# Linear attention and SwiGLU block: q kept transposed, z by one-column matmuls, the reciprocal denominators broadcast through DRAM

## The chip, the cores and the metric

The kernel runs on one core of a Trainium2 chip. The metric is the device time in microseconds (us) of one execution; smaller is better. Inside a core, TensorE (PE) multiplies matrices into PSUM, VectorE (DVE), ScalarE (ACT) and GpSimd (POOL) do the elementwise work, and the queue of SyncE (SP) issues the DMAs. Each engine takes its instructions in program order and waits on semaphores for the others.

## The reference

S = 2048 tokens, D = 1024, 32 heads of 32, F = 3584; all tensors are bfloat16.

```python
mod = (silu(c) @ w_mod).reshape(1, 6, 1, -1)      # sa, ca, ga, sb, cb, gb
h = layernorm(x) * (1 + ca) + sa
q, k, v = split(h @ wqkv)                          # 32 heads of 32
phi = lambda t: where(t > 0, t + 1, exp(t)) + 1e-06
pq, pk = phi(q), phi(k)
kv  = einsum('bhsd,bhse->bhde', pk, v)
z   = einsum('bhsd->bhd', pk)                      # sum of pk over the tokens
num = einsum('bhqd,bhde->bhqe', pq, kv)
den = einsum('bhqd,bhd->bhq', pq, z) + 1e-06
x = x + ga * ((num / den) @ wo)
h = layernorm(x) * (1 + cb) + sb
x = x + gb * ((silu(h @ w_gate) * (h @ w_up)) @ w_down)
```

## The kernel before

Tokens come in 16 tiles of 128 (`NST`) and four chunks of 512 (`NCH`); D comes in eight tiles of 128 (`NDT`, `NHG`; one `hg` holds four heads). The order of the work is written out by hand: calls append instructions to each engine's list, dependences are found from the addresses, and each engine runs its list in order. All instructions are recorded by one helper, so every row of the profile has line L178 and has to be told apart by its tiles.

**Chunk 0** computes q in eight groups (`q_phase_chunk0`, line 623), then k in eight. Each group is eight matmuls into one PSUM bank and then `phi_evac` (line 556): ACT writes exp (`E1`, tile e) and relu (`RL`, tile rl), DVE takes min and adds (two instructions). Between the k groups of chunk 0 PE transposes chunk 1's normalised rows (`th_round`, line 459), four rounds with two ACT evacuations each.

**Chunks 1 to 3** (`chunk`, line 681) run 16 groups each. A table `side` hangs further work behind each group: the LayerNorm statistics, `ln1_rstd` and `ln1_xn` of a coming chunk (DVE, POOL), its DMA transposes into `HT` (`th_dma`, line 469), its modulation on ACT (`th_mod`, line 474, tile ht), and one-column matmuls of w_mod (`mod_col_mm`, line 594) whose result `mod_col_fin` spreads (`MODREP`) and `mod_bcast` (line 612) multiplies out to all partitions. `zacc` (line 585) adds each k tile to `PKSUM` in fp32 on DVE; after chunk 3 `PKSUM` is split into `ZHI` and `ZLO`, and four matmuls with a matrix of ones give `ZB`, z on all partitions.

**The G stage** (lines 816 to 849) computes G = xn^T · pk in 16 groups of 16 matmuls over four PSUM banks (`g_group`, 2 to 5), each evacuated by `g_evac` (ACT scales z into `GTMP`, DVE adds). Beside it the denominators of 16 token tiles are made, one per group: `den_prod` multiplies q by `ZB` on POOL, `den_scale` on DVE sums 32 columns each, adds 1e-6, takes the reciprocal, multiplies q by it, and has a DMA transpose q into `PQT`. `fold_ga` (DVE) multiplies `WO` by ga. `kvt_mm` makes v^T·k per head from G (PE, masked by DVE into `KVT`), `m_mm` multiplies it with `WO` into `MW`; both come in two halves, the second behind the last G group.

**The wo stage** (`wo_part`, `wo_res`, lines 804 to 902) multiplies `PQT` with `MW` for 16 token tiles and adds x, which is loaded again behind the G stage (`xr` DMAs, since `XRES` held the normalised rows). **The SwiGLU stage** follows.

Of the kernel before, what the change touches and what calls it, by code (L numbers as in the profile page):

```python
# [264 lines left out]
def bass_adaLN_cond__linear_attn_block__swiglu_ffn__prompt_kernel(  # L265
# [22 lines left out]
    with ExitStack() as es:  # L288
# [15 lines left out]
        PQ = T("pq", 32 * KB, [128, NST, D], BF16)  # L304
        WMSC = T("wmsc", 32 * KB, [128, NDT, 2048], BF16)
        AT = T("at", 32 * KB, [128, NFT, 512], BF16)
# [20 lines left out]
        DEN = T("den", SM + 2304, [128, 2, 32], FP32)  # L327
        RECIP = T("recip", SM + 2560, [128, 2, 32], FP32)
# [5 lines left out]
        PQT = T("pqt", 72 * KB, [128, NHG, S], BF16)  # L334
# [10 lines left out]
        PKSUM = T("pksum", 192 * KB, [128, D], FP32)  # L345
        ZHI = T("zhi", 184 * KB, [128, D], BF16)
        ZLO = T("zlo", 186 * KB, [128, D], BF16)
        GTMP = T("gtmp", 184 * KB, [128, 2, 512], FP32)
        KVT = T("kvt", 188 * KB, [128, NHG, 128], BF16)
        ZB = T("zb", 196 * KB, [128, D], FP32)  # L350
        PROD = [T("prod0", 192 * KB, [128, D], FP32), T("prod1", 200 * KB, [128, D], FP32)]
        WD_A = T("wd_a", 72 * KB, [128, 16, D], BF16)
# [14 lines left out]
        PS = nc.alloc_psum_tensor("ps", [128, 8, 512], FP32)  # L367
        PSB = PS.bitcast(BF16)

# [39 lines left out]
        for h in range(4):  # L409
            P.dve("memset", ap=MASK[32 * h:32 * h + 32, 32 * h:32 * h + 32], constant=1.0)  # L410

# [3 lines left out]

        def xnat(st):
            return XRES[:, st, :]
# [51 lines left out]
        def th_dma(ch):  # L469
            buf = ch % 2  # L470
            for j in range(4):
                xbar(HT[:, buf, :, j * 128:(j + 1) * 128], XRES[:, 4 * ch + j, :])
# [92 lines left out]
        def q_part(g, bank, dts):  # L565
            h, j = g // 4, g % 4
            for dt in dts:
                P.pe("matmul", out=PS[:, bank, :], lhsT=HT[:, 0, dt, j * 128:(j + 1) * 128],
                     rhs=WQK[:, dt, h * 512:(h + 1) * 512], start=(dt == 0), stop=(dt == NDT - 1))
# [4 lines left out]
        def qk_group(ch, j, isk, h):  # L574
            st = 4 * ch + j
            buf = ch % 2
            bank = QK_BANKS[qk_ctr[0] % 5]
            qk_ctr[0] += 1
            lo = isk * D + h * 512
# [3 lines left out]
            phi_evac(bank, PKH[h][:, st, :] if isk else PQ[:, st, h * 512:(h + 1) * 512])  # L583

        def zacc(st, h):
            dst = PKSUM[:, h * 512:(h + 1) * 512]
            if st == 0:
                P.dve("tensor_copy", out=dst, in_=PKH[h][:, st, :])
            else:
                P.dve("tensor_tensor", out=dst, in0=dst, in1=PKH[h][:, st, :], op=ALU.add)  # L590
# [3 lines left out]
        def mod_col_mm(piece, kt):  # L594
            c0 = 8 * piece
            for m in range(NDT):
                P.pe("matmul", out=PS[:, 6, c0 + m:c0 + m + 1], lhsT=STG[:, kt, m * 128:(m + 1) * 128],
                     rhs=SILUC[:, kt:kt + 1], start=mcol_first[0], stop=(kt == NDT - 1), skip_group_check=True)
                mcol_first[0] = False
# [23 lines left out]
        def q_phase_chunk0(side):  # L623
# [18 lines left out]
            for g in range(7):  # L642
                q_part(g, 1 + g, hi)
                phi_evac(1 + g, PQ[:, g % 4, (g // 4) * 512:(g // 4 + 1) * 512])
                for f in side.get(g, []):
                    f()
            q_part(7, 1, lo + hi)
            phi_evac(1, PQ[:, 3, 512:1024])
# [14 lines left out]
        for jj in range(4):  # L663
            add(kside, jj // 2, lambda jj=jj: ln1_xn(4 + jj))
        for r in range(4):
            add(kside, 3 + r, lambda r=r: th_round(1, r, 7 if r % 2 == 0 else 6, "act"))
        q_phase_chunk0(qside)
        gi = 0
        for h in range(2):
            for j in range(4):  # L670
                qk_group(0, j, 1, h)
# [3 lines left out]
            for j in range(4):  # L675
                add(kside, 100 + h, lambda j=j, h=h: zacc(j, h))
        for h in range(2):
            for f in kside[100 + h]:
                f()

        def chunk(ch, side):
            gi = 0
            for j in range(4):
                st = 4 * ch + j
                for (isk, h) in [(0, 0), (1, 0), (0, 1), (1, 1)]:
                    qk_group(ch, j, isk, h)
                    for f in side.get(gi, []):
                        f()
                    if isk:
                        zacc(st, h)  # L690
                    gi += 1
# [20 lines left out]
        for i, f in enumerate(ops):  # L712
            add(s1, 8 + (i * 2) // 3, f)
# [4 lines left out]
        add(s2, 0, lambda: ln1_rstd(3))  # L718
        for jj in range(4):
            add(s2, 1 + jj // 2, lambda jj=jj: ln1_xn(12 + jj))  # L720
        add(s2, 2, lambda: th_dma(3))
        for dt in range(NDT):
            add(s2, 8 + dt, lambda dt=dt: th_mod(3, dt))
        piece_mm(s2, 1, 0)
        add(s2, 7, lambda: mod_col_fin(1, 3, False, False))
        add(s2, 7, lambda: stg_load(2))
        piece_mm(s3, 2, 0)
        add(s3, 7, lambda: mod_col_fin(2, 2, True, False))
        add(s3, 7, lambda: stg_load(3))
# [29 lines left out]
        def den_prod(st):  # L759
            P.pool("tensor_tensor", out=PROD[st % 2][:], in0=PQ[:, st, :], in1=ZB[:], op=ALU.mult)  # L760

        def den_scale(st):
            i = st % 2
            P.dve("tensor_reduce", out=DEN[:, i, :], in_=PROD[i][:].rearrange("p (h e) -> p h e", e=32),
                  axis=mybir.AxisListType.X, op=ALU.add)
            P.dve("tensor_scalar", out=DEN[:, i, :], in0=DEN[:, i, :], scalar1=1e-6, scalar2=None, op0=ALU.add)
            P.dve("reciprocal", out=RECIP[:, i, :], in_=DEN[:, i, :])
            P.dve("tensor_tensor", out=PQ[:, st, :].rearrange("p (h e) -> p h e", e=32),
                  in0=PQ[:, st, :].rearrange("p (h e) -> p h e", e=32),
                  in1=RECIP[:, i, :].unsqueeze(2).to_broadcast([128, 32, 32]), op=ALU.mult)  # L770
            xbar(PQT[:, :, st * 128:(st + 1) * 128], PQ[:, st, :])

# [42 lines left out]

        g_group(0)
        for h in range(2):
# [171 lines left out]
```

## Time and profile before

| | |
|---|---|
| three runs | 895.74 us median (895.6 to 896.42) |
| the profiled execution, own time | 895.89 us |
| its span, first to last instruction | 894.1 us |
| mean granted TensorE clock | 0.977 |
| SwiGLU stage | from 311.2 us to the end |

The trace is of one execution. Its view by windows gives the busy time of each engine in a stretch, its timeline each instruction's start and length with the idle time before it and what ended that, its groups the mean length of one instruction of a kind, and its DMA list the time from issue to landing. "Granted clock" is the share of the full TensorE clock that the chip allowed.

### The profile page before, as it was taken

To read this page: it belongs to the slowest core of one execution; us is meant where nothing else is said; L and a number is where in the kernel's file an instruction comes from. 1 tells how busy PE (TensorE), PEld (TensorE's weight loads), DVE (VectorE), ACT (ScalarE), POOL (GpSimd) and SP (SyncE) were. 2 spreads that over 40 slices of the span, in tenths; PEclk is the share of its full clock that TensorE was granted. 3 is DMA by queue.
4 is the path that set the end of the run, shared out by engine and by line. 5 is a ranking of instruction groups with operands and counts; after the bars stand their busy time and mean duration, and the time that the engine had idled before them with its cause. 6 is when DMAs were issued, how large, how long until landed. Compare 5 with 4: busy or idle time off the path is not lost.

```text
span 894.1 us, 10474 instructions
## 1 busy us (share of the span) xinstructions
PE 843.3 (94%) x4289; PEld 391.3 (44%) x4289; DVE 329.5 (37%) x638; ACT 220.2 (25%) x375; POOL 69.2 (8%) x66
## 2 busy tenths in 40 slices
PE   4897899966779999999999999999999999999998
PEld 3453345433334444444444444444444444444444
DVE  4658655699975422121112121112212111212111
ACT  4664685311123321111111111111111111111101
POOL 1000000333300300002000000200000200000000
PEclk9988999997979999999999999999999999999999
DMA  9924432312255779655025556204555602554000
GB/s 302 376 76 100 84 101 95 107 36 57 42 138 154 196 239 306 187 142 152 22 61 141 156 164 158 64 18 134 154 142 145 150 24 59 143 162 119 1 24 24
DMA packets 185233, 110.80 MB, mean 124 GB/s; under 512 B 44896, under 2 KB 170848, under 8 KB 185184
## 3 DMA queue, kind: packets, MB, share of 16 engines
q1 hardware_dynamic: 185184, 110.12, 44.0%
q8 instruction: 34, 0.56, 0.3%
q14 instruction: 15, 0.12, 0.0%
HBM read 95.42 MB, written 4.19 MB: 111 GB/s over the span
## 4 chain that ended last, share of the span: by engine, by line
PE 80%; DVE 9%; issue 5%; ACT 4%; DMA 1%; SPq 0%; POOL 0%; DVEq 0%; ACTq 0%
PE ps L178 80%; DVE den L178 2%; ACT e_89 L178 1%; ACT ht L178 1%; ACT rl L178 1%; DMA wmsc<-in_w_mod_dram 1%; DVE g L178 1%; DVE stats L178 1%; DVE pksum L178 1%; DVE recip L178 1%; DVE wo L178 1%; DVE pq L178 1%; DVE xres L178 1%; DVE mw L178 0%; DVE e_89 L178 0%
## 5 line engine op out<-in xcount | busy, mean ns | idle before, releaser
L178 DVE TENSOR_TENSOR at<-sg,ps 128x512 bf16<-128x512 bf16 x112 | 77.0, 687 | 300.0 <-PE ps L178 298.3
L178 ACT ACTIVATE sg<-ps 128x512 bf16<-128x512 f32 x112 | 66.9, 597 | 310.5 <-PE ps L178 310.5
L178 PE MATMUL ps<-wqk,ht 128*128 128x512 bf16 x512 | 124.4, 395 | 3.3 <-ACT ht L178 3.3
L178 PE MATMUL ps<-wd_a,at 128*128 128x512 bf16 (+2 forms) x528 | 115.9, 373 | 0.0
L178 PE MATMUL ps<-wd_b,at 128*128 128x512 bf16 (+2 forms) x396 | 88.3, 373 | 0.0
L178 PEld LDWEIGHTS ps<-wd_a,at 128*128 128x128 bf16 x528 | 51.1, 98 | 59.8
L178 PEld LDWEIGHTS ps<-wqk,ht 128*128 128x128 bf16 x512 | 49.2, 101 | 61.9 <-issue 8.4
L178 DVE TENSOR_TENSOR ut<-att,gb_b 128x512 bf16<-128x512 bf16 (+1 forms) x32 | 14.5, 454 | 164.8 <-ACT att L178 164.8
L178 ACT ACTIVATE att<-ps 128x512 bf16<-128x512 f32 (+1 forms) x32 | 19.0, 594 | 179.7 <-PE ps L178 179.7
L178 PE MATMUL ps<-mw,pqt 128*128 128x512 bf16 x256 | 57.0, 383 | 1.0 <-DVE xres L178 1.0
L178 PEld LDWEIGHTS ps<-wd_b,at 128*128 128x128 bf16 x396 | 38.3, 98 | 44.7
L178 POOL TENSOR_SCALAR h2t<-h2t,modcol 128x512 bf16<-128x512 bf16 x32 | 25.0, 797 | 394.6 <-DMA h2t<-xn_110 394.6
L178 PE MATMUL ps<-h2t,gug_102 128*128 128x512 bf16 x224 | 52.9, 379 | 0.0
L178 PE MATMUL ps<-h2t,guu_106 128*128 128x512 bf16 x224 | 52.9, 379 | 0.0
L178 PE MATMUL ps<-h2t,gug_103 128*128 128x512 bf16 x224 | 52.9, 379 | 0.0
L178 PE MATMUL ps<-h2t,guu_108 128*128 128x512 bf16 x224 | 52.9, 379 | 0.0
L178 PE MATMUL ps<-h2t,gug_105 128*128 128x512 bf16 x224 | 52.9, 379 | 0.0
L178 PE MATMUL ps<-h2t,guu_109 128*128 128x512 bf16 x224 | 52.9, 379 | 0.0
L178 PE MATMUL ps<-h2t,guu_107 128*128 128x512 bf16 x224 | 52.9, 379 | 0.0
L178 PE MATMUL ps<-h2t,gug_104 128*128 128x512 bf16 x224 | 52.9, 379 | 0.0
L178 ACT ACTIVATE e_89<-ps 128x512 bf16<-128x512 f32 x64 | 38.6, 603 | 40.5 <-PE ps L178 30.9
L178 DVE TENSOR_TENSOR pq<-pq,recip 128x1024 bf16<-128x1024 bf16 x16 | 40.6, 2536 | 0.6
(104 smaller groups left out, 716.3 us busy)
## 6 DMA issues: line engine op xcount, KB each, us to landing
stg<-in_w_mod_dram SPq DMA_DIRECT2D x4, 2048.0 KB, 8.0
gug_102<-in_B_w_gate_dram SPq DMA_DIRECT2D x14, 512.0 KB, 3.9
guu_106<-in_B_w_up_dram SPq DMA_DIRECT2D x14, 512.0 KB, 5.1
gug_103<-in_B_w_gate_dram SPq DMA_DIRECT2D x14, 512.0 KB, 4.0
guu_107<-in_B_w_up_dram SPq DMA_DIRECT2D x14, 512.0 KB, 5.2
gug_104<-in_B_w_gate_dram SPq DMA_DIRECT2D x14, 512.0 KB, 3.9
guu_108<-in_B_w_up_dram SPq DMA_DIRECT2D x14, 512.0 KB, 5.2
gug_105<-in_B_w_gate_dram SPq DMA_DIRECT2D x14, 512.0 KB, 3.9
```

The source lines that it names most:

```text
L178: return getattr(e, method)(**kw)
```

## The change

Five parts belong together. `PQT` becomes the place where q is computed: in `q_group` the weight `WQK` is the stationary operand and `HT` the moving one, so q comes out transposed, and `phi_evac` writes it there; `PQ` and 16 DMA transposes go. z becomes 128 one-column matmuls (`z_mm`, `PKH` against a column of ones, into PSUM bank 6), in place of `zacc`; `z_bcast` spreads it to all partitions. `den` computes all denominators with 32 matmuls of 32 output rows each (`ZSEL` picks the four heads of a group), one add, one reciprocal and one cast on DVE, writes 32x2048 reciprocals to a DRAM scratch (four DMAs), waits for them on SP, and reads them back spread over the partitions into `RB` (four DMAs of 1 MB in SBUF). `scale_pq` multiplies `PQT` by `RB` in eight DVE instructions. The chunks do their eight k groups first and then the eight q groups, and the LayerNorm work, transposes and modulation get other places in the side tables. `AT` and `WD_A` change places in SBUF with it.

```diff
-        def th_dma(ch):
...
+        def th_dma(st):
+            buf, j = (st // 4) % 2, st % 4
+            xbar(HT[:, buf, :, j * 128:(j + 1) * 128], XRES[:, st, :])
...
+        def q_group(ch, nt):
+            buf, bank = ch % 2, next_bank()
+            for dt in range(NDT):
+                P.pe("matmul", out=PS[:, bank, :], lhsT=WQK[:, dt, nt * 128:(nt + 1) * 128],
+                     rhs=HT[:, buf, dt, :], start=(dt == 0), stop=(dt == NDT - 1))
+            phi_evac(bank, PQT[:, nt, ch * 512:(ch + 1) * 512])
...
-        def zacc(st, h):
...
+        def z_mm(st):
+            for hg in range(NHG):
+                P.pe("matmul", out=PS[:, 6, 32 + hg:33 + hg], lhsT=PKH[hg // 4][:, st, (hg % 4) * 128:(hg % 4 + 1) * 128],
+                     rhs=ONES[:, 0:1], start=mcol_first[0], stop=(st == NST - 1), skip_group_check=True)
                 mcol_first[0] = False
...
-            add(kside, jj // 2, lambda jj=jj: ln1_xn(4 + jj))
+            add(kside, 1 + jj // 2, lambda jj=jj: ln1_xn(4 + jj))
         for r in range(4):
-            add(kside, 3 + r, lambda r=r: th_round(1, r, 7 if r % 2 == 0 else 6, "act"))
+            add(kside, 4 + r, lambda r=r: th_round(1, r, 7 if r % 2 == 0 else 6, "act"))
...
         def chunk(ch, side):
-            gi = 0
-            for j in range(4):
-                st = 4 * ch + j
-                for (isk, h) in [(0, 0), (1, 0), (0, 1), (1, 1)]:
-                    qk_group(ch, j, isk, h)
...
-                    if isk:
-                        zacc(st, h)
-                    gi += 1
+            for gi in range(16):
+                if gi < 8:
+                    k_group(ch, gi // 2, gi % 2)
+                else:
+                    q_group(ch, gi - 8)
+                for f in side.get(gi, []):
+                    f()
...
+        for j in range(4):
+            add(s1, 1 + j, lambda j=j: z_mm(j))
+            for ch, s_ in ((1, s1), (2, s2), (3, s3)):
+                add(s_, 4 + 2 * j, lambda st=4 * ch + j: z_mm(st))
...
-            add(s1, i // 2, f)
-        add(s1, 6, lambda: ln1_rstd(2))
+            add(s1, (i * 5) // 12, f)
+        add(s1, 4, lambda: ln1_rstd(2))
         for jj in range(4):
             add(s1, 6 + jj // 2, lambda jj=jj: ln1_xn(8 + jj))
-        add(s1, 7, lambda: th_dma(2))
-        for dt in range(NDT):
-            add(s1, 12 + dt // 2, lambda dt=dt: th_mod(2, dt))
+            add(s1, 6 + jj // 2, lambda jj=jj: th_dma(8 + jj))
+        for i, dt in zip([10, 11, 11, 12, 12, 13, 13, 14], range(NDT)):
+            add(s1, i, lambda dt=dt: th_mod(2, dt))
...
-        add(s1, 7, lambda: mod_col_fin(0, None, False, True))
-        add(s1, 7, lambda: stg_load(1))
-        add(s1, 9, lambda: mod_bcast(GA_B))
...
+        add(s1, 8, lambda: mod_col_fin(0, None, False, True))
+        add(s1, 8, lambda: stg_load(1))
+        add(s1, 13, lambda: mod_bcast(GA_B))
...
-            add(s2, 8 + dt, lambda dt=dt: th_mod(3, dt))
+            add(s2, 7 + dt, lambda dt=dt: th_mod(3, dt))
...
-            add(s3, 12 + kt // 2, lambda kt=kt: mod_col_mm(3, kt))
-        add(s3, 15, lambda: mod_col_fin(3, None, False, True))
+            add(s3, 14 + kt // 4, lambda kt=kt: mod_col_mm(3, kt))
...
-        P.dve("tensor_copy", out=ZHI[:], in_=PKSUM[:])
-        P.dve("tensor_tensor", out=ZLO[:], in0=PKSUM[:], in1=ZHI[:], op=ALU.subtract)
+        P.dve("tensor_copy", out=ZCOL[:], in_=PS[:, 6, 32:40])
+        P.dve("tensor_copy", out=ZHL[:, 0, :], in_=ZCOL[:])
+        P.dve("tensor_tensor", out=ZHL[:, 1, :], in0=ZCOL[:], in1=ZHL[:, 0, :], op=ALU.subtract)
...
+        for i in range(2):
+            P.dve("tensor_copy", out=ZREP[:, i, :, :], in_=ZHL[:, i, :].unsqueeze(2).to_broadcast([128, NHG, 128]))
+        mod_col_fin(3, None, False, True)
...
+        def z_bcast():
+            for h in range(2):
+                for hl in range(4):
+                    for i in range(2):
+                        P.pe("matmul", out=PS[:, h, hl * 128:(hl + 1) * 128], lhsT=ZREP[:, i, 4 * h + hl, :],
+                             rhs=IDENT[:], start=(hl == 0 and i == 0), stop=(i == 1), skip_group_check=True)
+                P.act("activation", out=ZB[:, h * 512:(h + 1) * 512], in_=PS[:, h, :], func=ACT.Copy)
+
+        def den():
+            for hg in range(NHG):
+                for ch in range(NCH):
+                    P.pe("matmul", out=PS[32 * ch:32 * ch + 32, 7, :], lhsT=ZSEL[:, hg * 32:hg * 32 + 32],
+                         rhs=PQT[:, hg, ch * 512:(ch + 1) * 512], start=(hg == 0), stop=(hg == NHG - 1),
+                         skip_group_check=True)
+            P.dve("tensor_scalar", out=DEN[:], in0=PS[:, 7, :], scalar1=1e-6, scalar2=None, op0=ALU.add)
+            P.dve("reciprocal", out=RCP[:], in_=DEN[:])
+            P.dve("tensor_copy", out=RCB[:], in_=RCP[:])
+            wr = [P.dma("rdr%d" % ch, RDR[:, ch * 512:(ch + 1) * 512], RCB[32 * ch:32 * ch + 32, :])
+                  for ch in range(NCH)]
+            P.wait_for("sp", wr)
+            for hh in range(4):
+                src = RDR.rearrange("(g x) s -> x g s", x=4)[hh].unsqueeze(0).to_broadcast([32, NHG, S])
+                P.dma("rb%d" % hh, RB[32 * hh:32 * hh + 32, :, :], src)
+
+        def scale_pq(hg):
+            P.dve("tensor_tensor", out=PQT[:, hg, :], in0=PQT[:, hg, :], in1=RB[:, hg, :], op=ALU.mult)
...
+        z_bcast()
         g_group(0)
...
         g_evac(0)
-        mod_bcast(GB_B)
-        den_prod(0)
+        den()
         for g in range(1, 16):
             g_group(g)
             g_evac(g)
-            if g < 15:
-                den_prod(g)
-            den_scale(g - 1)
...
+            if g == 2:
+                mod_bcast(GB_B)
+            if 3 <= g <= 6:
+                fold_ga(2 * g - 6)
+                fold_ga(2 * g - 5)
+            if g == 9:
                 kvt_mm(0)
...
+            if 11 <= g <= 14:
+                m_mm(g - 11, [0, 1, 7])
+            if 8 <= g <= 15:
+                scale_pq(g - 8)
```

On PE, at the k groups of chunk 0, before (`ident,xres` are the transposes of chunk 1's rows; eight rows `wqk,ht` are one group, the first row of 80 ends with four k groups):

```order
L178 MATMUL ps<-wqk,ht 128x512 x80
L178 MATMUL ps<-ident,xres 128x128 x8
L178 MATMUL ps<-wqk,ht 128x512 x8
L178 MATMUL ps<-ident,xres 128x128 x8
L178 MATMUL ps<-wqk,ht 128x512 x8
L178 MATMUL ps<-ident,xres 128x128 x8
L178 MATMUL ps<-wqk,ht 128x512 x8
L178 MATMUL ps<-ident,xres 128x128 x8
L178 MATMUL ps<-wqk,ht 128x512 x16
L178 MATMUL ps<-siluc,stg 128x1 x8
```

and now (`ht,wqk` is a q group):

```order
L178 MATMUL ps<-ht,wqk 128x512 x48
L178 MATMUL ps<-wqk,ht 128x512 x40
L178 MATMUL ps<-ident,xres 128x128 x8
L178 MATMUL ps<-wqk,ht 128x512 x8
L178 MATMUL ps<-ident,xres 128x128 x8
L178 MATMUL ps<-wqk,ht 128x512 x8
L178 MATMUL ps<-ident,xres 128x128 x8
L178 MATMUL ps<-wqk,ht 128x512 x8
L178 MATMUL ps<-ident,xres 128x128 x8
L178 MATMUL ps<-wqk,ht 128x512 x8
```

Five k groups stand ahead of the first round instead of four, and none stands behind the last round: the row that follows it is chunk 1's first group, which reads what that round transposed.

On PE, from the end of chunk 3 into the G stage, before (`siluc,stg` are one-column matmuls of w_mod, `pk,xres` G groups):

```order
L178 MATMUL ps<-siluc,stg 128x1 x16
L178 MATMUL ps<-pk_84,xres 128x512 x16
L178 MATMUL ps<-zhi,ones 128x512
L178 MATMUL ps<-zlo,ones 128x512
L178 MATMUL ps<-zhi,ones 128x512
L178 MATMUL ps<-zlo,ones 128x512
L178 MATMUL ps<-ident,modrep 128x128 x8
L178 MATMUL ps<-pk_84,xres 128x512 x112
L178 MATMUL ps<-pk_85,xres 128x512 x16
L178 MATMUL ps<-g,wv 128x128 x32
```

and now (`ident,zrep` is `z_bcast`, `pqt,zsel` is `den`):

```order
L178 MATMUL ps<-siluc,stg 128x1 x32
L178 MATMUL ps<-ident,zrep 128x128 x16
L178 MATMUL ps<-pk_85,xres 128x512 x16
L178 MATMUL ps<-pqt,zsel 32x512 x32
L178 MATMUL ps<-pk_85,xres 128x512 x32
L178 MATMUL ps<-ident,modrep 128x128 x8
L178 MATMUL ps<-pk_85,xres 128x512 x80
L178 MATMUL ps<-pk_86,xres 128x512 x32
L178 MATMUL ps<-g,wv 128x128 x32
```

The spreading of z moved from behind the first G group to ahead of it, the 32 denominator matmuls are new, and the first `g,wv` (kvt_mm) stands behind ten G groups instead of nine.

On DVE, in the G stage, before (the work of one of the early groups; the later ones lack the two `wo` rows):

```order
L178 SCALAR_TENSOR_TENSOR g<-ps,modcol,gtmp 128x512
L178 TENSOR_REDUCE den<-prod_99 128x32
L178 TENSOR_SCALAR den<-den 128x32
L178 RECIPROCAL recip<-den 128x32
L178 TENSOR_TENSOR pq<-pq,recip 128x1024
L178 TENSOR_TENSOR wo<-wo,ga_b 128x1024 x2
```

and now, from the evacuations of groups 7 and 8 on (counted from 0):

```order
L178 SCALAR_TENSOR_TENSOR g<-ps,modcol,gtmp 128x512 x2
L178 TENSOR_TENSOR pqt<-pqt,rb 128x2048
L178 SCALAR_TENSOR_TENSOR g<-ps,modcol,gtmp 128x512
L178 TENSOR_TENSOR kvt<-ps,mask 128x512
L178 TENSOR_TENSOR pqt<-pqt,rb 128x2048
L178 SCALAR_TENSOR_TENSOR g<-ps,modcol,gtmp 128x512
```

Four denominator instructions per group are gone; one multiplication of 2048 columns stands behind each of the last eight evacuations, and the first of them stands ahead of the mask of kvt.

More of the change, by code (lines that the diff above doesn't have):

```diff
@@ L641, in q_phase_chunk0 @@
             q_part(6, 7, lo)
[L642 to L645, printed above, removed]
+            for nt in range(7):
+                q_part(nt, 1 + nt, hi)
+                phi_evac(1 + nt, PQT[:, nt, 0:512])
+                for f in side.get(nt, []):
                     f()
             q_part(7, 1, lo + hi)
-            phi_evac(1, PQ[:, 3, 512:1024])
+            phi_evac(1, PQT[:, 7, 0:512])
             for f in side.get(7, []):
@@ L814, in wo_res @@
                   op1=ALU.add, accum_out=SUMXH[:, st, nh:nh + 1])
+        z_bcast()
         g_group(0)
-        for h in range(2):
-            for (zt, s0, s1_) in [(ZHI, True, False), (ZLO, False, True)]:
-                P.pe("matmul", out=PS[:, h, :], lhsT=ONES[:], rhs=zt[:, h * 512:(h + 1) * 512], start=s0, stop=s1_)
-            P.act("activation", out=ZB[:, h * 512:(h + 1) * 512], in_=PS[:, h, :], func=ACT.Copy)
         g_evac(0)
-        mod_bcast(GB_B)
-        den_prod(0)
+        den()
         for g in range(1, 16):
```

108 lines of the change are left out of this document (41 added, 67 removed).

## The prediction

> **What bounds the kernel now.** I read the page's engine line first, then the windows cut at the stages, then PE's waits.
>
> ```profile
> PE 843.3 (94%) x4289; PEld 391.3 (44%) x4289; DVE 329.5 (37%) x638; ACT 220.2 (25%) x375; POOL 69.2 (8%) x66
> core 0: us, PE busy (x) PEld busy (x) DVE busy (x) ACT busy (x) POOL busy (x), PEclk, DMA share, GB/s
> 58.41:98.70 40.29, 32.72 (x201) 15.18 (x200) 33.74 (x80) 23.71 (x42) 1.01 (x1) 0.92 0.34 79
> 193.30:208.50 15.20, 3.61 (x33) 3.10 (x32) 14.89 (x18) 2.17 (x3) 5.67 (x3) 0.65 0.27 52
> 311.17:894.10 582.93, 580.39 (x2717) 264.54 (x2715) 113.98 (x197) 88.29 (x147) 20.02 (x25) 1.00 0.43 119
> PE ps L178 <- DVE g L178: 20.6, 5, 4.9
> PE ps L178 <- DVE modrep L178: 5.0, 1, 5.0
> PE ps L178 <- ACT ht L178: 3.3, 6, 1.3
> ```
>
> PE at 94% is an average that hides two places. From 311 us to the end PE has almost no gap, and the change adds nothing there: those 583 us stay. From 193 to 208 us, in the G stage, DVE is busy for 14.9 of 15.2 us and PE for 3.6; PE waits 20.6 us in all for DVE's evacuations of G. In chunk 1 (58 to 99 us) DVE is busy for 33.7 of 40.3 us, and PE waits 5.0 us for `MODREP`.
>
> ```profile
> 175.72 0.74 DVE L178 SCALAR_TENSOR_TENSOR g<-ps,modcol,gtmp 128x512 bf16<-128x512 f32 x1
> 176.38 1.20 DVE L178 TENSOR_REDUCE den<-prod_99 128x32 f32<-128x1024 f32 x1
> 178.23 2.73 DVE L178 TENSOR_TENSOR pq<-pq,recip 128x1024 bf16<-128x1024 bf16 x1
> 182.08 0.74 DVE L178 SCALAR_TENSOR_TENSOR g<-ps,modcol,gtmp 128x512 bf16<-128x512 f32 x1
> 165.70 24.34 PE L178 MATMUL ps<-pk_84,xres 128*128 128x512 bf16 x112
> 189.87 3.62 PE L178 MATMUL ps<-pk_85,xres 128*128 128x512 bf16 x16
> ```
>
> From one evacuation to the next DVE takes 6.36 us. PE takes (189.87 - 165.70) / 112 = 0.216 us per matmul, 3.45 per group. PE runs ahead through its four banks until `kvt_mm` wants the last evacuations; then it stands.
>
> **G stage -17.5, tail -13.2.**
>
> ```profile
> 54.51 0.61 PE L178 MATMUL ps<-ident,xres 128*128 128x128 bf16 x8
> 54.95 3.62 PE L178 MATMUL ps<-wqk,ht 128*128 128x512 bf16 x16
> 238.56 1.89 PE L178 MATMUL ps<-mw,pqt 128*128 128x512 bf16 x8
> 311.17 1.89 PE L178 MATMUL ps<-h2t,gug_102 128*128 128x512 bf16 x8
> ```
>
> Behind 165.70 stand 240 G matmuls (51.8 us), 32 of `kvt_mm` at (54.95 - 54.51) / 8 = 0.055 (1.8) and eight of `m_mm` (1.7): 55.3 us of work in the 72.9 up to 238.56, so 17.5 lost, to waits and to the lowered clock that they bring (0.65 above). From 238.56 to 311.17, 72.6 us, stand 256 wo matmuls, 32 and eight: 58.8. I leave 0.6 for bank and mask waits between the last `m_mm`; 13.2 go.
>
> They go only if DVE keeps up and `RB` is there in time.
>
> ```profile
> L178 DVE TENSOR_TENSOR wo<-wo,ga_b 128x1024 bf16<-128x1024 bf16 x8 | 5.1, 679 | 0.0
> L178 DVE RECIPROCAL recip<-den 128x32 f32<-128x32 f32 x16 | 5.6, 353 | 0.6
> L178 DVE TENSOR_SCALAR den<-den 128x32 f32<-128x32 f32 x16 | 2.9, 182 | 0.6
> L178 DVE CAST mw<-ps 128x512 bf16<-128x512 f32 x8 | 5.5, 685 | 2.7 <-PE ps L178 2.6
> stg<-in_w_mod_dram SPq DMA_DIRECT2D x4, 2048.0 KB, 8.0
> out_dram<-xres SPq DMA_DIRECT2D x31, 128.0 KB, 1.7
> 254.29 2.00 SPq L178 DMA_DIRECT2D xres<-in_A_x_dram  x4
> ```
>
> DVE, groups 8 to 15: evacuation 0.74, `scale_pq` of 2048 columns at 2 x 0.68 = 1.4 (same form as the `wo` row; at most 2 x 2.73, the `pq` row, which ran beside POOL's products, and these are gone), a cast 0.69: 2.8 of 3.45. Groups 3 to 6: 0.74 + two `fold_ga`, 2.1. So DVE has room; at 2.7 per `scale_pq` the four groups with a cast would cost 0.7 each, 2.7 in all.
>
> `RB`: the reciprocal of 512 columns is 0.69 + 512 x (353 - 182) / 32 ns = 3.4 us (between 0.69 and 16 x 0.353 = 5.6). Add before it 0.7 and cast behind it 0.4 make 4.5. Four write issues at 0.5 and a landing of 1.7 (SP stands in its wait; behind it are only the `RB` loads and the x loads, which wait for the last G group anyway) make 3.7. The loads write 4.2 MB: at 2 MB in 8.0 us, 16.0. Together 24.2 us behind `den`. `scale_pq(0)` comes up after groups 1 to 8, the GB broadcast and one evacuation, 28.8 behind `den`; and PE feels a late one only at `m_mm(0)`, whose mask stands behind it on DVE, 9.4 us later. Hidden, with 14 us to spare; the loads may take 29 us.
>
> **The denominators: +6.9.** No row has a 32-row matmul. Matmul time in the rows follows the moving columns (0.216 for 512, 0.055 for 128), so 32 of 512 columns cost 6.9; if the four of one set, which write different quarters of a bank, ran side by side, 8 x 0.216 = 1.7. I take the upper end, the row's own pace; both ends stay in the range.
> The Trainium skill, "TensorE: Matmul & The Clock Gate", Part 3 on packing small matmuls, states that matmuls with 32 output rows in different column groups run at the same time, three of them 2.38 times as fast. No run here shows it yet; an estimate from that page is 6.9 / 2.38 = 2.9.
>
> **z: +3.2, and the wait for it +2.1 and +1.7.**
>
> ```profile
> 60.33 0.34 PE L178 MATMUL ps<-siluc,stg 128*128 128x1 bf16 x8
> 60.54 1.89 PE L178 MATMUL ps<-wqk,ht 128*128 128x512 bf16 x8
> 159.17 0.60 ACT L178 ACTIVATE e_89<-ps 128x512 bf16<-128x512 f32 x1 [1.04 <-PE ps L178]
> 160.63 0.16 DVE L178 CAST modtmp<-ps 128x8 bf16<-128x8 f32 x1
> 160.82 0.69 DVE L178 COPY modrep<-modtmp 128x1024 bf16<-128x1024 bf16 x1
> 160.31 3.63 PE L178 MATMUL ps<-pk_84,xres 128*128 128x512 bf16 x16 [0.86 <-ACT rl L178]
> 95.40:98.70 3.30, 1.38 (x4) 0.40 (x5) 2.35 (x6) 3.03 (x5) 0.00 (x0) 1.00 0.00 0
> 98.70:102.30 3.60, 3.60 (x18) 1.38 (x17) 0.80 (x3) 1.09 (x2) 1.01 (x1) 0.53 0.00 0
> ```
>
> Eight one-column matmuls take 0.21 us, and the same form is issued 128 times: 16 x 0.2 = 3.2 on PE. `zacc` goes from DVE. The spreading matmuls (16 x 0.055) replace four of 0.216: nothing. But they now stand ahead of the first G group and need `ZREP`, the end of a DVE chain behind the last q group: 1.46 us from its exp to the next DVE instruction (159.17 to 160.63), four small ones at 0.2, two copies at 0.69 (both needed by the second matmul): 3.7 us, of which 32 one-column matmuls cover 0.8. PE stands for 3.0 where it stood for 0.86, +2.1. After idling 1.9 of 3.3 us PE ran the next 3.6 at clock 0.53; I charge the same, 3.6 x 0.47 = 1.7 (0 if the clock holds).
> The Trainium skill, the same page, Part 1 on the clock gate, has the clock halved after an idle window of about 3.4 us; by that rule 3.0 us would cost nothing. The two rows above halve it sooner, so the trace does not agree.
>
> **Chunks: -1.4, -5.0, -1.9.**
>
> ```profile
> 43.31 0.22 PE L178 MATMUL ps<-ident,xres 128*128 128x128 bf16 x1 [1.99 <-DVE xres L178]
> 45.83 3.62 PE L178 MATMUL ps<-wqk,ht 128*128 128x512 bf16 x8
> 58.41 0.34 PE L178 MATMUL ps<-siluc,stg 128*128 128x1 bf16 x8
> 52.59 0.60 ACT L178 ACTIVATE e_89<-ps 128x512 bf16<-128x512 f32 x1 [0.69 <-PE ps L178]
> 54.89 0.61 ACT L178 ACTIVATE e_89<-ps 128x512 bf16<-128x512 f32 x1
> 80.70:84.50 3.80, 3.77 (x15) 1.86 (x16) 3.59 (x9) 1.08 (x2) 0.00 (x0) 0.50 1.17 126
> ht<-xres SPq DMA_TRANSPOSE x8, 4.6
> ```
>
> In chunk 0 the fifth k group (1.7) fills the hole in front of the transposes, which DVE's normalised rows end at 45.8 as before. But no k group is left behind the fourth round, so chunk 1's first group, done at 58.41 now, waits for ACT at 2.3 us per round (52.59 to 54.89). Counting rounds from 45.8 it is done between 55.7 (full clock) and 57.4 (half clock at first, as in the 45.83 row, 3.4 us for eight matmuls): -2.7 to -1.0. PE still idles over 2 us there, so I take -1.4.
> In chunk 1, 16 `zacc` of about 0.6 leave DVE, 10 of its 33.7 us, and `mod_bcast` stands five groups behind `MODREP` instead of two: its 5.0 goes, and the 3.8 us at clock 0.50 behind it (1.9). The 3.3 us for ACT at the start of chunk 2 I leave (-3.3 to +2): `th_mod` moves two groups up, but two per group on ACT (2.4 us against PE's 1.73) and the transposes' 4.6 us of landing leave ACT as late as before.
>
> **Sum.** -17.5 - 13.2 + 6.9 + 3.2 + 2.1 + 1.7 - 1.4 - 5.0 - 1.9 = -25.1, against the profiled execution's own 895.9 (span 894.1): 870.8. The median of the runs is 0.15 below that execution: 870.6.
>
> **Rivals.**
> 1. *Denominators side by side*: 1.7 in place of 6.9 gives 865.4. For it: four matmuls write separate partitions. Against it: no two matmuls overlap in any row. The skill's packing rule is the same case.
> 2. *Late RB, still faster*: reading each row of the scratch 32 times at 100 GB/s takes 42 us; 13 beyond the 29 that are hidden give 883.6.
> 3. *Slower*: the same loads, on DVE at `scale_pq(0)`, from where every microsecond past 29 is one of PE's. Gain is gone at 29 + 25 = 54 us, 78 GB/s; at 64 GB/s, 66 us, the time is 907. For it: small transfers do move at that rate (128 KB in 1.7 us, 77 GB/s). Against it: that is landing time, and 2 MB go at 262.
> 4. *LayerNorm work doesn't come free* (the change doesn't do what it says): DVE's wait for `MODREP` turns into one for the modulated rows of chunk 2, and the 6.9 of chunk 1 stay: 877.5.
>
> **Chances.** Forecast 0.42, rival 1 0.37, rival 2 0.08, rival 3 0.04, rival 4 0.09. Range: down to 859 (rival 1 with full clock and no wait at chunk 2), up to 884, which takes in rivals 2 and 4. Faster by over 0.2% (about what a measurement can tell from no change): 0.95; within 0.2%: 0.01; slower: 0.04.
>
> **What would show it.** Right: no PE wait for `g` over 1 us in the G stage, G groups at 3.45 us, first wo matmul some 60 us ahead of the SwiGLU stage, `pksum` gone and `modrep` waits gone, one wait of 3 us for `zrep`. The 32 `zsel` matmuls show 7 us or 2. Wrong: DVE waiting for DMA `rb`, PE waiting for `kvt` or `mw` in the G stage, or a SwiGLU stage longer than 583 us.

## The result and the profile after

The changed kernel takes 859.69 us (median of four runs, 858.00 to 860.61), the kernel before in the same comparison 895.88 (895.60 to 896.42). The ratio is 0.9593, 95% interval 0.9576 to 0.9611. The profiled execution is the quickest of the four: own time 858.0, span 856.0, granted clock 1.0. In spans it gained 38.1 us.

First the engine line on the page of the changed kernel's profile, then its view of PE's waits (us in total, times, longest).

```profile
PE 834.7 (98%) x4461; PEld 390.3 (46%) x4461; DVE 257.8 (30%) x563; ACT 219.9 (26%) x375; POOL 35.3 (4%) x50
```

```profile
PE ps L178 <- DMA wmsc<-in_w_mod_dram: 8.9, 3, 7.9
PE ps L178 <- ACT ht L178: 2.8, 4, 1.8
PE ps L178 <- DVE zrep L178: 2.5, 2, 2.1
PE ps L178 <- DMA cs_56<-in_c_dram: 2.2, 1, 2.2
PE ps L178 <- DVE xres L178: 1.9, 4, 1.0
PE ps L178 <- ACT mw L178: 0.5, 2, 0.3
```

The 20.6 us for `g` and the 5.0 for `modrep` are gone. DVE's busy time fell by 72 us and POOL's by 34. One wait is new, `zrep`. Next the windows of the changed kernel, cut at the same instructions as before (chunk 1, the G stage from its first group, the wo stage, SwiGLU).

```profile
core 0: us, PE busy (x) PEld busy (x) DVE busy (x) ACT busy (x) POOL busy (x), PEclk, DMA share, GB/s
55.36:88.62 33.26, 31.45 (x266) 16.06 (x265) 23.84 (x61) 22.80 (x41) 1.01 (x1) 1.00 0.35 96
...
152.24:213.40 61.16, 61.16 (x339) 28.78 (x337) 31.23 (x38) 14.97 (x24) 0.00 (x0) 1.00 0.40 101
213.40:273.13 59.73, 59.21 (x298) 27.37 (x297) 30.98 (x88) 19.41 (x34) 9.03 (x11) 1.00 0.55 149
273.13:856.00 582.87, 580.39 (x2717) 264.54 (x2715) 113.74 (x197) 88.30 (x147) 20.17 (x25) 1.00 0.43 119
```

In the G stage PE is now busy for all of 61.16 us and DVE for half of them. Before, DVE was the full one there. SwiGLU is where it was, to 0.1 us. The rows at which the stages begin come from PE's timeline (start, length, instruction, idle time before it and what ended that).

```profile
55.36 0.34 PE L178 MATMUL ps<-siluc,stg 128*128 128x1 bf16 x8
...
88.39 0.39 PE L178 MATMUL ps<-wqk,ht 128*128 128x512 bf16 x1 [1.81 <-ACT ht L178]
88.62 0.34 PE L178 MATMUL ps<-siluc,stg 128*128 128x1 bf16 x8
...
118.64 0.34 PE L178 MATMUL ps<-siluc,stg 128*128 128x1 bf16 x8
...
150.79 0.23 PE L178 MATMUL ps<-ident,zrep 128*128 128x128 bf16 x1 [2.11 <-DVE zrep L178]
151.40 1.01 PE L178 MATMUL ps<-ident,zrep 128*128 128x128 bf16 x15 [0.37 <-DVE zrep L178]
152.24 3.62 PE L178 MATMUL ps<-pk_85,xres 128*128 128x512 bf16 x16
155.79 1.91 PE L178 MATMUL ps<-pqt,zsel 128*32 128x512 bf16 x32
157.63 2.55 PE L178 MATMUL ps<-pk_85,xres 128*128 128x512 bf16 x11
...
197.86 0.59 PE L178 MATMUL ps<-wo,kvt 128*128 128x512 bf16 x2
...
213.40 1.89 PE L178 MATMUL ps<-mw,pqt 128*128 128x512 bf16 x8
...
273.13 1.89 PE L178 MATMUL ps<-h2t,gug_103 128*128 128x512 bf16 x8
```

The stages against the forecast, all in us. The starts of before are the rows that the prediction quotes, and these two from the same timeline of PE, where the first groups of chunks 2 and 3 end:

```profile
98.71 0.34 PE L178 MATMUL ps<-siluc,stg 128*128 128x1 bf16 x8
130.21 0.34 PE L178 MATMUL ps<-siluc,stg 128*128 128x1 bf16 x8
```

| stretch | before | after | change | forecast |
|---|---|---|---|---|
| to the end of chunk 1's first group | 58.41 | 55.36 | -3.05 | -1.4 |
| to the end of chunk 2's first group | 40.30 | 33.26 | -7.04 | -5.3 (-5.0 - 1.9 + 1.6 for z) |
| to the end of chunk 3's first group | 31.50 | 30.02 | -1.48 | +0.8 (z) |
| to the first wo matmul | 108.35 | 94.76 | -13.59 | -6.0 (-17.5 + 6.9 + 2.1 + 1.7 + 0.8) |
| wo stage | 72.61 | 59.73 | -12.88 | -13.2 |
| SwiGLU | 582.93 | 582.87 | -0.06 | 0 |
| sum | | | -38.1 | -25.1 |

More than half of what the forecast missed (7.6 of 13.0) lies in the fourth row. There the 32 `zsel` matmuls took 157.63 - 155.79 = 1.84 us and not 6.9, and the G matmuls behind the wait for `zrep` ran at the full pace (152.24, 16 in 3.55).

Three more views of the changed kernel: DVE's timeline, SyncE's timeline, and the DMA list (the last number is the median time from issue to landing).

```profile
158.48 3.35 DVE L178 RECIPROCAL rcp<-den 128x512 f32<-128x512 f32 x1
...
192.71 1.23 DVE L178 TENSOR_TENSOR pqt<-pqt,rb 128x2048 bf16<-128x2048 bf16 x1 [6.04 <-DMA rb<-recip_den]
193.85 0.75 DVE L178 SCALAR_TENSOR_TENSOR g<-ps,modcol,gtmp 128x512 bf16<-128x512 f32 x1
194.51 0.68 DVE L178 TENSOR_TENSOR kvt<-ps,mask 128x512 bf16<-128x512 f32 x1
```

```profile
162.32 1.73 SPq L178 DMA_DIRECT2D recip_den<-rcb  x4
165.28 20.94 SPq L178 DMA_DIRECT2D rb<-recip_den  x4
```

```profile
rb<-recip_den SPq DMA_DIRECT2D x4, 1024.0 KB, 6.9
```

The four `RB` loads are not in flight together. Their issues spread over 20.94 us, each as long behind the one ahead as a load takes to land (6.9): the program's search for dependences goes by the addresses inside a partition, takes the four loads, which write different partitions, for writes to one place, and has SP wait for each. They last from 165.3 to 192.7, 27.4 us. DVE waits 6.0 us for them, but PE first feels it at `m_mm(0)` (197.86), and the mask in front of that is done at 194.51 + 0.68 = 195.2: hidden, with 2.7 us to spare. DVE waiting for `rb` is one of the prediction's own signs of being wrong, and it did show; it cost PE nothing, since what was left of the margin covered it.

### The profile page after: what moved, and what is told of

The parts are those of the page before. It is cut to its first block, busy times and chain, and to the rows that moved or that the text cites. A ratio compares the mean times of both kernels' runs of the same rounds, so it can differ in the third digit from the quotient of the medians.

```text
span 856.0 us, 10690 instructions
## 1 busy us (share of the span) xinstructions
PE 834.7 (98%) x4461; PEld 390.3 (46%) x4461; DVE 257.8 (30%) x563; ACT 219.9 (26%) x375; POOL 35.3 (4%) x50
## 4 chain that ended last, share of the span: by engine, by line
PE 93%; ACT 2%; DMA 2%; SPq 1%; DVE 1%; issue 0%; ACTq 0%
PE ps L178 93%; DMA wmsc<-in_w_mod_dram 2%; SPq L178 1%; ACT ht L178 1%; ACT rl L178 1%; ACT e_90 L178 1%; DMA ht<-xres 0%; DVE zrep L178 0%; ACT mw L178 0%; DVE xres L178 0%; ACT ga_b L178 0%; DVE pqt L178 0%; DVE stats L178 0%; DVE pk_85 L178 0%; DVE zhl L178 0%
## 5 line engine op out<-in xcount | busy, mean ns | idle before, releaser
L178 PE MATMUL ps<-wqk,ht 128*128 128x512 bf16 x256 | 60.3, 379 | 2.5 <-ACT ht L178 2.5
L178 PE MATMUL ps<-ht,wqk 128*128 128x512 bf16 x256 | 59.2, 386 | 0.3 <-ACT ht L178 0.3
L178 ACT ACTIVATE e_90<-ps 128x512 bf16<-128x512 f32 x64 | 38.7, 604 | 34.5 <-PE ps L178 30.7
L178 PEld LDWEIGHTS ps<-mw,pqt 128*128 128x128 bf16 x256 | 25.0, 98 | 29.7
```

The costliest lines, as they stand in the source:

```text
L178: return getattr(e, method)(**kw)
```

## The experiments

The theory after the result: every part did what the prediction said except the `zsel` matmuls, and the extra 13 us are (a) their overlap, (b) half-clock stretches that the prediction kept or added and that this execution did not have, and (c) some shorter waits. The rivals: the `RB` loads, the places in the side tables rather than the work taken from DVE, and chance in the clock. Kernels of one batch ran on one chip beside the kernel before (893.85, 893.93 and 894.38 us in the three batches, in the table's order e0 to e7, e3 to e6, e9 to e11); a difference from e0 across batches is one of medians.

| run | what it is | median us | ratio to before, interval |
|---|---|---|---|
| e0_after_again | the changed kernel | 859.48 | 0.9616 [0.9600, 0.9633] |
| e1_den_serial | other order of the `zsel` matmuls | 862.22 | 0.9650 [0.9629, 0.9670] |
| e2_zb_behind | z spread behind the first G group | 857.15 | 0.9590 [0.9577, 0.9603] |
| e7_rb_parallel | the four `RB` loads at once | 862.08 | 0.9632 [0.9610, 0.9654] |
| e3_rb_twice | `RB` loaded twice | 889.41 | 0.9955 [0.9938, 0.9971] |
| e4_before_no_den | before, without denominators | 864.36 | 0.9669 [0.9654, 0.9684] |
| e5_before_no_zacc | before, z over one token tile | 888.21 | 0.9936 [0.9919, 0.9953] |
| e6_old_slots | changed, old places in the side tables | 868.02 | 0.9708 [0.9694, 0.9723] |
| e9_zwait_k1 | `ZREP` copied twice | 862.51 | 0.9646 [0.9622, 0.9670] |
| e10_zwait_k3 | `ZREP` copied four times | 865.09 | 0.9676 [0.9650, 0.9703] |
| e8_best | e2 and e7 together, GA broadcast later | 856.29 | 0.9579 [0.9554, 0.9604] |
| e11_best2 | e8 with some ACT work on DVE | 855.78 | 0.9569 [0.9545, 0.9594] |

The first batch repeats the changed kernel, as the measure for the others:

> The changed kernel itself, for comparison with the three beside it: 859.7 us as before (858.0 to 860.6 in four runs).

Its four runs read 858.11 at a mean clock of 1.0, 859.20 and 859.75 at 0.998, 861.21 at 0.996: the scatter of this kernel goes with the granted clock, about 1.5 us for each 0.002. The four runs of the result show the same less evenly: 858.00 and 858.99 at 1.0, 860.40 at 0.998, 860.61 at 0.996.

**Do the `zsel` matmuls overlap?** If they do because neighbours write different quarters of a bank, an order in which neighbours write the same quarter takes that away.

```diff
-            for hg in range(NHG):
-                for ch in range(NCH):
+            for ch in range(NCH):
+                for hg in range(NHG):
```

> The 32 denominator matmuls in another order: eight in a row write the same quarter of the bank, where before each wrote another quarter than the one ahead of it. Theory: matmuls that write different quarters run side by side (32 took 1.84 us in the changed kernel, 0.058 each); in the new order each needs 0.216, 6.9 in all, and the time grows by 5.1 us. Rival: a matmul with 32 output rows is cheap in any order; the 32 stay at 1.8 us and the time doesn't change.

PE's timeline of e1, the row of the 32 and the one behind it:

```profile
156.69 4.54 PE L178 MATMUL ps<-pqt,zsel 128*32 128x512 bf16 x32
161.16 3.19 PE L178 MATMUL ps<-pk,xres 128*128 128x512 bf16 x14
```

4.47 us (161.16 - 156.69) in place of 1.84, and the time rose by 2.7; the two intervals touch, but at equal clocks e1 is above e0 too, 860.56 against 858.11 at 1.0. That the order changes the pace shows that the overlap is real and hangs on which quarter is written. The 5 us that full serialisation would cost did not come. A count that fits: eight in a row on one quarter go one at a time, but the next quarter starts after four of them, 3 x 4 x 0.216 + 8 x 0.216 = 4.3. Windows of 0.1 us, cut to the `zsel` instructions, bear it out (PE busy and the matmuls in hand, PEld, DVE, PEclk, DMA share, GB/s):

```profile
156.90:157.00 0.10, 0.10 (x2) 0.08 (x1) 0.00 (x0) 1.00 0.00 0
159.10:159.20 0.10, 0.10 (x4) 0.09 (x1) 0.00 (x0) 1.00 0.00 0
160.80:160.90 0.10, 0.10 (x2) 0.00 (x0) 0.00 (x0) 1.00 0.00 0
```

About two matmuls are in hand until 157.5, three to six from there to 160.3, and two again at the end, where the changed kernel has mostly eight or more: first one quarter at work, then two, then one. The ends of matmuls are modelled in these views, and why the next quarter starts after four is not shown.

**What does the wait for `zrep` cost?** In e2 the spreading of z goes behind the first G group, so DVE's chain has 3.5 us of cover. In e9 and e10 the same wait is made longer by copying `ZREP` two and four times.

```diff
-        z_bcast()
         g_group(0)
+        z_bcast()
```

```diff
-        for i in range(2):
+        for i in (0, 1, 0, 1):
             P.dve("tensor_copy", out=ZREP[:, i, :, :], in_=ZHL[:, i, :].unsqueeze(2).to_broadcast([128, NHG, 128]))
```

> The spreading of z stands behind the first G group instead of ahead of it, as in the kernel before. Theory: PE's wait for zrep (2.1 + 0.4 us) is hidden behind the group's 3.45 us, and the time falls by 2.5 us. Rival: the wait moves on to the first evacuation of G or to the denominators, and the time stays within 0.5 us.

> The two copies into ZREP are done twice, so PE's hole ahead of the spreading of z grows from 2.5 to 3.8 us. Theory (a hole of this length lets the clock drop in most executions, one of 2.5 only in some): the time grows by 1.3 us for the wait and by up to 2 for the half clock, and the granted clock of nearly every run is 0.998 or less: 2 to 3 us above the changed kernel. Rival: the clock doesn't depend on this hole; 1.3 us.

> The copies into ZREP four times: the hole grows to 6.4 us. Theory: the clock drops in every execution and PE runs 3 to 4 us at half clock behind the hole: 3.9 us for the wait and 1.5 to 2 for the clock, 5.5 to 6 above the changed kernel. Rival: 3.9 alone.

From PE's timeline of e2; then PE's wait and a window behind the hole, of e9 and after it of e10 (columns as in the windows above):

```profile
150.45 3.63 PE L178 MATMUL ps<-pk,xres 128*128 128x512 bf16 x16 [0.46 <-ACT rl L178]
153.91 1.06 PE L178 MATMUL ps<-ident,zrep 128*128 128x128 bf16 x16
```

```profile
PE ps L178 <- DVE zrep L178: 3.7, 2, 3.3
```

```profile
154.00:158.00 4.00, 3.11 (x20) 2.15 (x21) 1.83 (x4) 1.74 (x4) 0.00 (x0) 0.66 0.97 368
```

```profile
PE ps L178 <- DVE zrep L178: 6.0, 2, 5.7
```

```profile
158.00:162.00 4.00, 4.00 (x12) 1.40 (x10) 0.00 (x0) 1.81 (x3) 0.00 (x0) 0.56 0.01 2
```

In e2 the 2.5 us of waiting are 0.46, for ACT; the time falls by 2.3, as expected. In e9 the wait is 1.2 longer and the time 3.0 over e0; in e10 3.5 longer and 5.6 over, both as expected: some 2 us more than the wait. The windows show half clock behind the hole, PE at 0.66 just behind it in e9 and at 0.56 as late as 158 to 162 in e10. What it costs is read from the first `zrep` matmul to the first `zsel` one, which is the same work in each: 5.00 us in the changed kernel, e0 and e1 (150.79 to 155.79 in the first), 6.66 in e9 and 7.54 in e10. So a half-clock term behind this wait exists. It does not need a longer wait: with the same 2.5 us the stretch takes 6.63 to 6.69 us in e3, e6 and e7, 1.7 more, and PE's clock is 0.57 to 0.68 there (windows of 4 us). Of six profiles with this wait three have the term and three have not. In e9's profile the clock is low at 43 to 56 and 85 to 92 us too, so its 2 us are not all from this hole; in e10's it is 1.00 in both places.

**Do the `RB` loads cost anything?** e7 issues the four loads as one operation (`rb_fn` holds the four `dma_start`); e3 loads `RB` twice, so that the cover is surely used up.

```diff
-                P.dma("rb%d" % hh, RB[32 * hh:32 * hh + 32, :, :], src)
+            P.add("sp", rb_fn, reads=[], writes=[RB[:]], lane="rb0", ninc=4, tag="rb")
```

```diff
-            for hh in range(4):
+            for hh in (0, 1, 2, 3, 0, 1, 2, 3):
```

> The four loads of RB are issued at once. In the changed kernel SP waits for each before it issues the next, since the program's dependence list goes by addresses within a partition and takes the four for writes to one place. Theory: the loads are hidden with 2.7 us to spare as they are (the mask of kvt is done at 195.2, and the last G group ahead of the first m_mm at 197.9), so the time doesn't change (within 0.5 us), while RB lands at least 8 us earlier and DVE's wait of 6.0 us for it goes. Rival: DVE's wait costs PE something, and the time falls by over 1 us. If the loads still take 27 us together, the bound is the transfer itself and not the waits between them.

> The four loads of RB are issued twice, each waiting for the one before: 55 us in place of 27.4. Theory (late RB): PE has 2.7 us to spare, so it waits 27.4 - 2.7 = 24.7 us at the first m_mm, and the clock may drop for some us behind that: the time grows by 25 to 29 us, to 885 to 889. Rival: the loads are hidden anyway, no change.

SyncE's timeline of e7, then DVE's, then a window behind the wait for `zrep`:

```profile
169.81 2.14 SPq L796 DMA_DIRECT2D rb<-recip_den  x4
```

```profile
192.09 1.22 DVE L178 TENSOR_TENSOR pqt<-pqt,rb 128x2048 bf16<-128x2048 bf16 x1 [0.90 <-DMA rb<-recip_den]
```

```profile
154.00:158.00 4.00, 3.77 (x23) 1.96 (x24) 0.94 (x3) 2.30 (x4) 0.00 (x0) 0.68 1.01 387
```

All four are issued within 2.14 us and are there after 192.09 - 169.81 = 22.3 us, 5 us less than one after the other. DVE's wait went from 6.0 to 0.9 and PE gained nothing, as a transfer that is hidden should. The median is 2.6 us above e0, where no change was expected; the intervals of the two overlap, and the clock accounts for it: four of the five runs have clock 0.994 and the fifth, at 1.0, took 857.70 against e0's 858.11 at 1.0. In the profiled run the low clock stands at 43 to 56 us, 85 to 92 and 154 to 158 (the last row, 0.68), all ahead of the first `RB` load, where the edit has changed nothing yet. Why this kernel drew more such stretches than e0 stays open.

PE's longest wait in e3, then its timeline:

```profile
PE ps L178 <- DVE kvt L178: 25.1, 1, 25.1
```

```profile
229.01 1.03 PE L178 MATMUL ps<-wo,kvt 128*128 128x512 bf16 x2 [25.08 <-DVE kvt L178]
229.84 6.14 PE L178 MATMUL ps<-pk,xres 128*128 128x512 bf16 x16
```

Loaded twice, PE stands 25.1 us, at the place the prediction named (the mask in front of `m_mm(0)`); 27.4 more of loading less the 2.7 spare would be 24.7. Behind it 16 matmuls take 6.14 in place of 3.62. The time is 29.9 above e0, just over the 25 to 29 expected: nearly the whole gain of the change hangs on these loads being covered.

**What was the denominators' work worth by itself?** e4 is the kernel before with the denominators left out altogether (neither products nor sums nor reciprocals, and q is not divided).

```diff
-            P.pool("tensor_tensor", out=PROD[st % 2][:], in0=PQ[:, st, :], in1=ZB[:], op=ALU.mult)
...
-            P.dve("tensor_scalar", out=DEN[:, i, :], in0=DEN[:, i, :], scalar1=1e-6, scalar2=None, op0=ALU.add)
-            P.dve("reciprocal", out=RECIP[:, i, :], in_=DEN[:, i, :])
...
```

> The kernel before with the denominators left out: no product on POOL, no sum, reciprocal and multiplication on DVE; q is transposed as it is, so the output isn't divided. Theory: these alone make the G stage and its tail slow; the time falls by the 30.7 us of the prediction's two terms, to 865. Rival: the evacuations, the order of kvt and the DMA transposes hold a good part of it (fall of 20 us or less).

One of PE's waits in e4:

```profile
PE ps L178 <- DVE modrep L178: 5.0, 1, 5.0
```

It takes 29.6 us off: the waits for `g` and `kvt` are no longer in the list, and that for `modrep` stays at 5.0. The G and wo terms of the prediction were 30.7.

**What cleared the chunks?** e5 is the kernel before with z summed over the first token tile alone (the 30 additions of the other 15 tiles are left out). e6 is the changed kernel with the LayerNorm work, the transposes, the modulation and the spreading of ga back at their old places in the side tables.

```diff
-                P.dve("tensor_tensor", out=dst, in0=dst, in1=PKH[h][:, st, :], op=ALU.add)
```

```diff
-            add(kside, 4 + r, lambda r=r: th_round(1, r, 7 if r % 2 == 0 else 6, "act"))
+            add(kside, 3 + r, lambda r=r: th_round(1, r, 7 if r % 2 == 0 else 6, "act"))
...
-            add(s1, 13, lambda: mod_bcast(GA_B))
+            add(s1, 9, lambda: mod_bcast(GA_B))
```

> The kernel before with z summed over the first token tile only (30 fp32 additions on DVE left out). Theory: these additions make DVE late in chunk 1; PE's wait for modrep (5.0) and the half clock behind it (1.9) go, 7 us in all, and DVE's chain ahead of the G stage gets shorter, under 1 us. Rival: the LayerNorm statistics alone keep DVE late: fall of 3 us or less.

> The changed kernel with the LayerNorm work, the transposes, the modulation and the spreading of ga at their old places in the side tables; z by matmuls and k ahead of q stay. Theory: with zacc gone from DVE the new places are worth only the fifth k group ahead of the transposes and a part of chunk 2's wait: the time grows by 2 to 5 us. Rival: the places are what brought the chunks' gain (10.8 us from the start of chunk 1 to the end of chunk 3): it grows by 8 or more.

One of PE's waits in e5, then three of e6:

```profile
PE ps L178 <- DVE modrep L178: 0.8, 1, 0.8
```

```profile
PE ps L178 <- DVE xres L178: 3.4, 3, 2.3
PE ps L178 <- ACT ht L178: 3.3, 6, 1.3
...
PE ps L178 <- DVE modtmp L178: 1.6, 1, 1.6
```

Without `zacc` alone the wait for `modrep` falls from 5.0 to 0.8 and the time by 5.7 (7 expected). The places count too: with the old ones the changed kernel loses 8.5 us, which is the rival's 8 or more and not the 2 to 5 expected. In e6's profile the first groups of chunks 1, 2 and 3 end at 59.20, 95.46 and 127.79 in place of 55.36, 88.62 and 118.64. Chunk 1's 7 us come about half from each: it takes 36.3 in e6, between 40.3 and 33.3. In e5 it takes 33.9 (56.67 to 90.53), 6.4 less than before; less the 1.6 that z costs PE there, this is 4.8 for the work taken from DVE, where e6 has 4.0. Chunk 2's gain comes from the places (32.3 in e6, 31.5 before). Chunk 0's gain is from the places as well, as far as it can be told, since this stretch scatters by itself: its end, 58.41 in the profile of before, is 57.98 in e4 and 56.67 in e5, whose instructions are the same up to there, and 55.04 to 57.93 in nine profiles of the changed kernel and its variants with the same instructions up to there (the middle one 56.32); e6's is 59.20.

**A better version.** e8 takes e2's and e7's edits and moves `mod_bcast(GA_B)` into chunk 2. e11 also has DVE do the last two of chunk 2's eight modulations and the evacuations of the last transpose round, since ACT ends the wait at that chunk's start.

```diff
-            add(s1, 13, lambda: mod_bcast(GA_B))
+            add(s2, 3, lambda: mod_bcast(GA_B))
...
+            if ch == 2 and dt >= 6:
+                P.dve("tensor_scalar", out=HT[:, buf, dt, :], in0=HT[:, buf, dt, :], scalar1=MODCOL[:, 0, dt:dt + 1],
```

> The changed kernel with z spread behind the first G group, the RB loads issued at once, and the spreading of ga moved from the end of chunk 1 to the fourth group of chunk 2, so that ACT's two copies for it leave the modulation that chunk 2 waits for. Theory: 2.3 us from z (measured alone), about 1.0 of the 1.8 us that PE waits at the start of chunk 2, nothing from RB: 3.3 us below the changed kernel, a ratio to the kernel before of about 0.958 where the changed kernel had 0.9616 in the same kind of run. Rival: only z's 2.3 us.

> As the one beside it, and two of the eight modulations of chunk 2 and the evacuation of the last round of chunk 1's transposes done on DVE instead of ACT. Theory: the rest of the wait at chunk 2 (0.8) and the wait at chunk 1 (0.7) go, and with them some of the stretches at half clock: 1.5 to 3 us below the one beside it. Rival: DVE is full there and passes the wait on; no change.

PE's waits of e11 (its profiled span is 852.9):

```profile
PE ps L178 <- DVE ht L178: 1.9, 2, 1.3
...
PE ps L178 <- ACT ht L178: 0.3, 1, 0.3
```

e8 is 3.2 us below e0 (3.3 expected); at chunk 2 its longest wait fell from 1.8 to 1.3, half of the 1.0 counted on there. e11 is the quickest of all, 855.78; its ratio's interval lies below e0's. Against e8 it is 0.5 us where 1.5 to 3 were expected, and the two intervals don't tell them apart: its rival, no change, fits as well; the wait for `ht` went from 2.3 in e8 to 2.2 in both rows together, so moving the modulation to DVE changed who is late rather than how late. Most of the gain over e0 is that of e2, the `zrep` wait taken away (2.3 of 3.7).

## Why the prediction was right, and where its sizes were off

The direction held, and each mechanism but one, the denominators one after the other; the sum was 13 us short. The measured 859.69 lies 0.7 us above the lower end of the range (859), nearer to rival 1 (865.4) than to the forecast (870.6), and two of the four runs, 858.00 and 858.99, lie at or below that end. By the prediction's own steps:

- **G stage -17.5, tail -13.2: right.** The G stage holds 61.16 us, and its work is 256 x 0.216 + 1.84 + 0.45 (the GB broadcast) + 1.8 + 1.7 = 61.1, so nothing is lost there now. The tail gave 12.9. e4 confirms the two terms from the other side (-29.6).
- **`RB` hidden: right, but the margin was mis-sized.** "16.0" for the loads was 27.4, since the prediction took the pace of a 2 MB load, which these do not reach even when issued together (22.3), and did not see that SP would wait between them. Of the 14 us to spare 2.7 were left, so that the loads stayed hidden is owed to the margin and not to their price; e3 shows what a late `RB` costs. The limit of 29 us was about right: the prediction's 16.0 + 14 make 30, and 27.4 + 2.7 measured make 30.1. The rates in rivals 2 and 3 (100 and 64 GB/s) are of no row; the loads ran at 153, and at 188 issued together. Reciprocal 3.35 (3.4 forecast), `scale_pq` 1.22 (1.4), first issue to first load 3.0 (3.7).
- **Denominators +6.9: the step that failed.** They cost 1.84, the 1.7 of the first rival, and e1 shows that it is the overlap. The prediction chose the pace of a full-width row because no row showed two matmuls at once; the kernel before had no matmul with 32 output rows, so its rows could not speak for or against it. The Trainium skill, "TensorE: Matmul & The Clock Gate", Part 3 on packing small matmuls, has such matmuls run at the same time, three of them 2.38 times as fast; here four went 3.75 times as fast as the row's pace (6.9, an estimate, against 1.84), so the trace agrees and goes further.
- **Half clock behind the wait for z, +1.7: the right size, and a matter of chance.** The profiled execution had none, so against it the forecast is 1.7 too long; three of the six profiles with this wait of 2.5 us have it, at 1.6 to 1.7 each. The same page of the Trainium skill, Part 1, has the clock drop after an idle window of about 3.4 us and calls that window free-running. That the same hole costs the clock in one execution and not in another agrees with a window that isn't tied to the kernel's work; that a hole of 2.5 us is enough does not agree with the 3.4.
- **The wait for z +2.1, z itself +3.2: right.** PE stands for 2.5 (3.0 forecast), and eight one-column matmuls take 0.20 (57.29 to 57.49 in its timeline).
- **Chunks -1.4, -5.0, -1.9: right in kind, too small in this execution.** Chunk 0 gave 3.05 between the two profiles. PE's windows behind the hole of this chunk, before and then in e0:

```profile
45.30:49.30 4.00, 3.98 (x14) 1.75 (x15) 1.22 (x4) 1.44 (x2) 0.00 (x0) 0.50 0.90 334
43.50:49.50 6.00, 4.64 (x25) 2.34 (x26) 3.17 (x9) 2.35 (x5) 0.00 (x0) 0.72 0.91 336
```

Before, the first matmuls behind the hole ran at clock 0.50; the changed kernel's profiled execution had 1.00 there, the full-clock end (-2.7) of the prediction's bracket, and e0, the same kernel, 0.72. By the middle ones of the profiles, 56.32 against 57.98 (before, e4 and e5), the gain is 1.7 and the 1.4 was right; the rest is the luck of the profiled execution. At chunk 2's start PE waits 1.81 where the prediction left 3.3, and no half-clock stretch follows, where before 98.70:102.30 stood at 0.53; the prediction saw both rows and left them in. The stretch is chance here too: behind the same wait e2's clock is 0.79 from 85 to 92 us and e7's 0.90.
- **Sum.** Denominators (5.1), wait for z and half clock behind it (2.2), chunk 0 (1.6) and chunks 1 and 2 (4.0) make 12.9 of the 13.0 by which the profiles differ from the forecast. By medians the miss is less, 36.2 against 25.1, since the profiled execution had no half-clock stretch and three of the four runs took 1 to 2.6 us longer.

That the denominators' overlap was the rival with nearly the forecast's own chance, and that the range reached down for it with full clock and no wait at chunk 2, kept the time inside the range, by a margin that is no larger than the scatter of the runs.

## What to carry to other kernels

Where a change brings an operation that no row shows, look for what is independent in it (here the four output quarters) before taking the pace of its dependent cousin, and order neighbours so that they stay independent. A transfer "hidden with 14 us to spare" deserves a check of whether its pieces run together or queue; its price is nothing up to the edge and then one for one, with half clock on top. When a wait of 2 us or more goes, count the half-clock stretch that may stand behind it as well as the wait: here 1.7 us in three of six profiled executions with 2.5 us of waiting, and more in the one with 6.0. And compare a stage in several profiles of the same instructions before calling a difference of 1 to 3 us the change's.

## What was not expected of the hardware

- Thirty-two matmuls of 32 output rows and 512 columns took 1.84 us with neighbours on different quarters of a bank, and 4.47 with eight in a row on the same quarter. The second is less than the 6.9 of one after the other, so quarters overlap across such runs too, by the count of matmuls in hand two at a time; how far ahead one may start was not tried by itself.
- Reading a DRAM scratch of 128 KB back spread to 4 MB ran at 4.19 MB / 27.4 us = 153 GB/s with loads one at a time and 188 GB/s with four at once, under the 262 of the plain 2 MB loads in the kernel before.
- The granted clock falls in some executions and not in others at the same wait of 1.8 us (chunk 2: 1.00 in the changed kernel's profile, 0.79 in e2) or 2.5 us (`zrep`: 1.00 in e0, 0.68 in e7), and the run-to-run scatter of this kernel goes with it: 858.1 to 861.2 us between clocks 1.0 and 0.996.
